# Attention scores issued two units at a time, their norms and transposes joined, and a new searched order of all instructions

## The chip, the cores and the metric

The kernel runs on one core of one Trainium2 chip. The metric is device time in microseconds (us), the median of several executions. The kernel before takes 306.1 us (306.01 to 306.51 in six runs, 0.2% apart).

Names used below: PE is TensorE's matmuls, PEld its weight loads, DVE is VectorE, ACT is ScalarE, POOL is GpSimd, SP is SyncE. "L482" is line 482 of the kernel's file. The changed kernel's lines are two higher for the same code; the experiments' lines are shifted by a few more.

## The reference, cut to what matters

Sliding-window attention with a linear bias, followed by a two-layer network with `h * cos(h)` between the layers:

```python
def _attn_ref(q, k, v):                       # 8 batches, 8 heads, 576 tokens, 64 per head
    scores = scale * np.matmul(q, k.transpose(0, 1, 3, 2))
    bias = slopes[:, None, None] * (-np.abs(rel))[None, :, :]
    mask = (rel >= 0) & (rel < 128)
    ...                                       # softmax over the masked scores
    return np.matmul(attn, v)

def _moe_ref(x, w_in, w_out):                 # 4608 tokens, 512 -> 2048 -> 512
    h = x @ w_in
    g = h * np.cos(h)
    return g @ w_out
```

## The kernel before: the parts that matter

The kernel records every operation with what it reads and writes, and then sorts them by a table of start times, `STARTS`. The order on each engine is therefore not the order of the source. The table was made by a search outside the file, and it also chooses the engine of those copies that two engines could do. Semaphore waits are derived from the recorded reads and writes.

```python
def schedule(self):
    raw, n = zlib.decompress(base64.b85decode(STARTS)), len(self.all)
    assert len(raw) == 2 * n
    code = 0
    for i, o in enumerate(self.all):
        code = (code + 256 * raw[i] + raw[n + i]) & 0xFFFF
        o.start = code >> 1
        if len(o.eng) > 1:
            e = "dve" if code & 1 else "act"
            o.fn, o.eng = o.fn[e], (e,)
    self.order = sorted(self.all, key=lambda o: (o.start, o.seq))
```

A unit is two heads by 256 queries. Its scores (K = 64) run in a TensorE tiling mode of 64 rows, everything else in the full array, or for the first transposes of q and k in 64 columns (the trace marks them 64\*128, 128\*128 and 128\*64). So each block of scores costs two changes of mode, measured below at 0.11 us each. After the scores come `exps` (ScalarE), `mask` (VectorE), `pv` (the products with v, TensorE), `norm` (VectorE: a reciprocal and a multiply) and `x_pe` (a transpose on TensorE and a copy).

```python
for n, u in enumerate(two):         # SINGLE = True: one unit's scores at a time
    scores([u], n)                  # banks SB[2n], SB[2n+1] of SB = [4, 5, 6, 7]
    exps(u, n, 2 * phase + 2)
    mask(u)
```

The softmax here doesn't subtract the row's maximum and nothing guards it: scores larger than these inputs give would overflow.

Of the kernel before, what the change touches and what calls it, by code (L numbers as in the profile page):

```python
# [14 lines left out]
B, H, S, D = 8, 8, 576, 64  # L15
# [12 lines left out]


STARTS = (  # L30
    "c-p;I3wTpS7S4^hPOtW3IEza=4J8h@wO<IOmTQ`1lBUHbq_qaD(3XObK9qJTg3wwN+^Q4{SV7CWu(niTzXjG+<RPGZDlcIHV"
    "dX>CU13+($G$#yeJ%(z$=$hmv`N!e*jL)jopa{QxpV$G=ReU1ilPa96#l3FYlNT}P?WGP_zf;bOhca`f=2izvaAVPs$(Ep5e"
    "Ujcl&JKG8jU~lK3|X9K+jCMYF+QlKZu=h#a^QQDLrDhFr=R-BiQv5XGHAr7>I;@A?ObYT5V9gc%7gKUuyb(0&yB8PUF|~|52"
    "h=L$CGsjIlO>E717+zl2^80)0RTL|yhkAcUM~eZsdIMNkHbWiUj9e+M*W05?|)nsNo2z~G<_QZNCbSM*1}J%Uwl1uETIRj1X"
    "cSZV|PVX1sKP*<6N!T>hfezDXJh^2pk8_*1(iA7t9E;%L8dmtsU&mZ!w@P{wDUIpc{x)9JR!lf`d__Y5E)P#7Ae-LDQXMNdG"
    "h{8|kSrwv+pg$%Q24zvrfP00$@kc<{1_IGH5JiHaNd#qW=yBm%)unJ*qYZWvpYUJ6xG#P}JjPK-#b-?f+t4w6!Ld6odwo}_`"
    "Hsv~`kt<rH5GqsC%LEzb?E;?8TW0({ejiP|Jq174OFxPX#!zQOj7l{A`Yt1uFL!x0p~wPp*xPIl(-h)i)$*E28hiUMQj5_>l"
    "<K~5Z4Wr_y7X2blTqyedk3BSJeCd$-mdcw0K_+U&p3Fe2*Kb-}U(+!CR7|RpL(K?{n_>^D6yBr3l?Iv4r?9&<_@Ye!NW{p$x"
    "I6r|Xkat=EWWu=pOr#+%*lJh!{+ughOZN?)|M;_ie`X9&&Dyr1;wKVHns%d=Vez}MaGWm_t$6!&d9hrvnqtx0+wo|an1CA;p"
    "D-Y9UEFRqr(!1OT((mt$s`YXA5O#Y0{tm>4_W9sC}iO-jfoDCPGM4};Q%~MUQ%Rm~va)ujaVUaw>=D@QA0TO>=zZK;YA|i91"  # L40
    "<F_J0A^}wO+(bYwB*F1a`<+~cC7^nC3>9H+fC!rhG6e+qk;TtI?F3XxbCcM5wATOxiAMW#NOgmdnXOSD{F^@aei6y)EU7U~U"
    "7RoeE@|=Yhz2c_nmW{n4T%|+1ZVes`O1`n#KWes*Lii@eo9s^|Cw%9C4N2WBk}-U?wOW3GQC<i_g3i)o@o2^=%IAOr1BNa!B"
    "Ln*juY*ssUtp^dMO8Al#&UMB=cG_-onH7sX)GczSg+ItIiTx?K<!C7^nwU%0R(d3K)vA%dtEk1C(O0O8iM_c0uU^z_PJGhar"
    "yw-bk}|gK<Ay0=S495U!>zf8;Yg+XaBFjsv(0+ARBwFTfDT;qv-|lKi`JZS}|5PypHOd<L+T%a-zYmE`Z@qinyC?<!`kKwbK"
    "dX<z{AybgO^#?8mzO-z5Y83WF0U4L&QVb6A$Ryg=&&LS66pVc`Jj;E6zziSc)A^+y{#AYsgw{7}%HR=SNhUB@bof|7JSyYi|"
    "NrTixhN&R5xZUmURlYa9H}0R`zRv7@;GSGWJi)sP4M{if;h>1fWMo!VaFYc^Evr|RT@)n&h$uNhO`@Qt0VEL_zOkH$+L1XNi"
    "{mUVG+e5QY!U&bSgbt!2x#xiRnW!?UunP@j)m@qE*o2sxeYeihw|{t*#>UoajfC?C)gf7n({li-o}0bUsK7x9oK^1-t2+g8H"
    "K~>Q5$uh<2Gjt?K_<0qvf}grpk(~riq5VnIG#Wot~At_QiX6=D@rK#a(XNw9oxoheO4XXAUZVa38GxzM4o}EPmD0NH(XQbe("
    "g8bobFwFz1NtVN*4I!f;?LzlB|$E2(><JF{lDH~FcqBlnuK+79IsM53|$l8^h<+z;!<9};81TrNLi<ydeG4Vfy~B1)OlYw%_"
    "f9iBCA!-S|U9NqMrEG2xJ71jV6j*=}lEMbW?^OB?%JCTdpEbqu}(6GW)vi_oD85F=2XE#qhgJT&5$Ym!vqD5>N9}Vmsjuy55"  # L50
    "O~$!=R1>*!wTo*eHenw&GsdAe73RP7Bw5<F`C)tB(J4de*L%yGN6@m7IUI*CIv=2Q{_OQ+Lw?Cik2Hfc?zC>tdmkMiV{K9kG"
    "~q`_QY%f4s@q&ScW~<`JI_|RSGpH8RC%xW4q1h)GqYx65(7%omz;;n)wxkZqSYuCE{rUi)Z9TRJ^O;nQCvACyeWBvsz9McuD"
    "P!!d*shuVRy!cEu6e~l8&4C7R^LbLr_u|?>saC5ap@Pv+xelAYz`xCia==;TM5O8@okBd9v6gmax}?T$We<5Sxt%-+^+mqcG"
    "^7LWZM>v!KYgNR9(Rs>4Rgt__;;bv6qjo4QI_Vvq@CsIoT_PN#fX@0`sQh!|lBQzJm&Zl`6paZYxrt1SO`*~#|%8~u{O{NWA"
    "7H7}nt9^0c<cuGyNYpE_Vb)o5&oZ+4Wr|aOBuXW8jR<)3f8P8EpsJYnUKIMM>pMI}|*I8#iHFg!hX=4aR;9(}c4%F77CTsAN"
    "Hq=xXlb1SFAs-1#7z)%}vz6^b!K72Q=E>Yk;V~<Bi|8vV%IWHmymJu-A{)gYw1+)?V$rGDW!V!X$YcP|N;bCy;2_I^<M1i_q"
    "yXq%KIa_3)&q9w?VAa~l-<mkG1I=3Q*a*J$!k4>P2z4STSKvncBJ46pe#kDQoD2c;iASJvv%FX<F=5~yDR3U(G@B4TnDAr&S"
    "F}*x?*Z^cN%sWaya{Sr7m6aMR5n2p2IV<we!!ZvviH?oWwGgV|shdljf>Zwbrb&e~INgNcsSfxrOxVo@kA+0I@jx^Qa9fs>#"
    "hUK8`+~Y}wr-+t8NsdNOV2j0pa#5Snm0(|Gr<0t7I%?+ijV3@A^+p<CdF49CzC;(N$37a&v5DzPM|v&Fn+$!t2eoLsmV8#%a"
    "-%6u=YBU^E%J;7KY>FdrL0HjOf3s!mP^fF?kMbp;O?M-bb>sIsdS9I>>g<jD#TBW<zPPg<hxrt+xv&@`zBGX!XDyRL&MowqZ"  # L60
    "WM&X|_k?7F#(WgRW*H^&-$esFhDt;#k|kd6OmX5#2pg<J(ghLKUvJr=iu1)#b%<5yGt2LT2Bcn`Pt*)Wdn}&E$qqep@_yN78"
    "O2dZXYU$8mgXM9Qucji-%@aW&+-!g`LW5qmN#HM8}DiHQ1%HvxQMcIKrd4^mU0By9krz{{a1;+X}`)wac}y=5B^Zb3s{vkD="
    "XJ~>Z$F)GZ0eB%bmADG5cdAx;pu<5b_v#2mv9ZT7wps+c()lVUp~Pk*W}R!xq7loQPEd?*U?Rq2)wx>V(M2vd9(7`)TZRp79"
    "y$&x0%<nRBBDpnknyHsN;mK3;Hi!rOZYHf^2ra<D)C2{1WhUkX&_T*3!F%7#+PzTzGV*cbE^p{$x$&H{D_Xq$;WxM(XB%*i%"
    "qrGodA?hS~^RM=mh;mQRn8oTOwMRsxBzVcrJ*4a4Kz6#+W)6W{LC?xQ4n;J;6=4k+<3yHb1+r!DL7RHSJL)xcd#|J}s56b9o"
    "NAC!~ZW|{Kb&{NRF701)z3_t"
)


# [150 lines left out]
def bass_alibi_sliding__then__act_gcu_kernel(  # L220
# [8 lines left out]
    with ExitStack() as ctx:  # L229
        def sb(name, shape, dt=BF16):  # L230
            return ctx.enter_context(nc.sbuf_tensor(name, shape, dt))

        R = Plan(nc, ctx)
# [7 lines left out]
        HF = NFC // 2  # L241
        T = {n: sb(f"wsum{n}", [128, HF, 256], F16) for n in (1, 2, 3, 4)}
# [9 lines left out]
        P = [sb(f"p{i}", [128, 2, 512]) for i in range(NP)]  # L252
        Pt = [sb(f"ptail{i}", [128, 1088]) for i in range(2)]
# [17 lines left out]
        SB, UB, OB = [4, 5, 6, 7], [2, 3], [0, 1]  # L271
# [634 lines left out]
            step("P4", "Y", False, (None, "p1", 2))  # L906
            step("P3", "Z", False, (None, "u2", 1))

        PAIRN = False
        SINGLE = True  # L910
        ucount = [0]

        def attention(us, phase):

            for g in range(0, len(us), 2):
                two = us[g:g + 2]
                if phase < 0 or SINGLE:
                    for n, u in enumerate(two):
# [66 lines left out]
        for c in range(NCH):  # L985
# [12 lines left out]
            n = QUOTA[c] if c < len(QUOTA) else 0  # L998
# [41 lines left out]
```

## Time and profile before

| | recorded profile of before | before, profiled again |
|---|---|---|
| span, us | 377.5 | 304.6 |
| time of that execution, us | 379.17 (slow state) | 306.34 (fast state) |
| PE / DVE / ACT busy | 97% / 69% / 55% | 96% / 83% / 67% |
| start to start, 512 columns | 266 or 318 ns | 216 ns |
| start to start, 256 columns | 110 or 159 ns | 109 ns |

These are the head of the recorded page, its chain of waits by engine, and two of its groups (line, engine, operation, tiles, shapes, count, then busy us and mean ns of one, then idle time before):

```profile
span 377.5 us, 7154 instructions
PE 365.6 (97%) x2882; PEld 228.0 (60%) x2900; DVE 260.7 (69%) x548; ACT 209.1 (55%) x298; POOL 95.1 (25%) x122
...
PE 96%; DMA 1%; ACT 1%; issue 1%; DVE 0%; ACTq 0%
...
L608 DVE TENSOR_TENSOR xnat<-ps,rec 128x256 bf16<-128x256 f32 x64 | 24.7, 419 | 0.3
L606 DVE RECIPROCAL rec<-ps 128x4 f32<-128x4 f32 x64 | 8.5, 168 | 18.5 <-PE ps L570 18.3
```

TensorE is the engine that bounds the kernel: 97% busy, 96% of the chain. But this execution took 379 us where plain ones take 306.

### The profile page before, as it was taken

How to read it: one execution, taken by the hardware profiler on the slowest of the kernel's cores; microseconds unless marked ns; L12 is line 12 of the kernel's file. 1: busy time of each engine (PE TensorE's matmuls, PEld its weight loads, DVE VectorE, ACT ScalarE, POOL GpSimd, SP SyncE). 2: the span in 40 equal slices, each digit the busy share in tenths (PEclk: the TensorE clock that was granted, in tenths of full speed). 3: DMA queues.
4: the chain of work that ended last, by engine and by line, in shares of the span. 5: the costliest groups of instructions: out<-in, count | busy, mean ns of one | idle time of the engine just before them, and what ended most of it. 6: DMA issues, size and time to landing. Idle time of an engine off the chain costs nothing.

```text
span 377.5 us, 7154 instructions
## 1 busy us (share of the span) xinstructions
PE 365.6 (97%) x2882; PEld 228.0 (60%) x2900; DVE 260.7 (69%) x548; ACT 209.1 (55%) x298; POOL 95.1 (25%) x122
## 2 busy tenths in 40 slices
PE   3999999999999999999999999999999999999997
PEld 2677445447753676447787765467645655554775
DVE  3976855568857877688757885787679654865743
ACT  6967655656646676558536862666456633445000
POOL 8992304196047002900490011000000000000000
DMA  8999999999989929990999389301220110100023
GB/s 150 182 211 203 168 181 130 133 124 157 149 117 156 109 37 158 171 93 28 114 160 180 52 92 136 88 10 37 55 77 2 43 21 28 44 13 0 30 84 113
DMA packets 148353, 38.09 MB, mean 101 GB/s; under 512 B 133984, under 2 KB 147040, under 8 KB 148320
## 3 DMA queue, kind: packets, MB, share of 16 engines
q0 software_dynamic: 99344, 18.10, 62.7%
q1 hardware_dynamic: 48976, 19.54, 25.6%
q8 instruction: 23, 0.38, 0.4%
q14 instruction: 10, 0.08, 0.1%
HBM read 36.70 MB, written 9.44 MB: 122 GB/s over the span
## 4 chain that ended last, share of the span: by engine, by line
PE 96%; DMA 1%; ACT 1%; issue 1%; DVE 0%; ACTq 0%
PE ps L712 38%; PE ps L853 34%; PE ps L482 5%; PE ps L797 5%; PE ps L736 5%; PE ps L567 3%; PE ps L570 2%; PE ps L429 2%; PE ps L674 1%; DMA ob<-in_q_dram 1%; ACT p L512 1%; PE ps L473 1%; PE ps L554 1%; PE ps L556 1%; DVE kt L445 0%
## 5 line engine op out<-in xcount | busy, mean ns | idle before, releaser
L712 PE MATMUL ps<-xT,w_inb 128*128 128x512 bf16 (+1 forms) x558 | 155.2, 429 | 1.6 <-DVE rec L606 0.2
L718 ACT ACTIVATE cos<-ps,halfpi 128x512 f32<-128x512 f32 x128 | 84.4, 686 | 83.8 <-PE ps L712 55.6
L722 DVE TENSOR_TENSOR gT<-ps,cos 128x512 f16<-128x512 f32 x128 | 85.0, 687 | 43.4 <-ACT cos L718 43.0
L712 PEld LDWEIGHTS ps<-xT,w_inb 128*128 128x128 bf16 x576 | 63.0, 111 | 65.4 <-issue 56.4
L512 ACT ACTIVATE p<-ps 128x768 bf16<-128x768 f32 (+1 forms) x64 | 56.3, 915 | 23.1 <-PE ps L482 16.1
L326 POOL DMA_DIRECT2D vp<-in_v_dram x40 | 33.8, 861 | 105.0 <-PE ps L570 87.6
L536 DVE TENSOR_TENSOR p<-p,emask 128x512 bf16<-128x512 bf16 (+2 forms) x96 | 42.4, 464 | 12.0 <-ACT p L512 11.0
L853 PE MATMUL ps<-wsum,gT 128*128 128x256 f16 x256 | 49.6, 319 | 0.0
L853 PE MATMUL ps<-wsum,gsum 128*128 128x256 f16 x256 | 47.7, 316 | 0.0
L853 PE MATMUL ps<-w_outb,gT 128*128 128x256 f16 x256 | 46.2, 319 | 0.3
L853 PEld LDWEIGHTS ps<-w_outb,gT 128*128 128x128 f16 x256 | 28.2, 111 | 12.2 <-issue 5.3
L853 PEld LDWEIGHTS ps<-wsum,gT 128*128 128x128 f16 x256 | 27.8, 112 | 10.0 <-issue 4.1
L853 PEld LDWEIGHTS ps<-wsum,gsum 128*128 128x128 f16 x256 | 27.1, 110 | 9.2 <-issue 2.8
L336 POOL DMA_DIRECT2D qnat<-in_q_dram x30 | 25.4, 887 | 15.7 <-DMA qt<-qnat 15.7
L336 POOL DMA_DIRECT2D knat<-in_k_dram x30 | 25.6, 915 | 11.5 <-DMA kt<-knat 9.3
L853 PE MATMUL ps<-w_outb,gsum 128*128 128x256 f16 x128 | 25.5, 320 | 0.0
L608 DVE TENSOR_TENSOR xnat<-ps,rec 128x256 bf16<-128x256 f32 x64 | 24.7, 419 | 0.3
L482 PE MATMUL ps<-qt,kt 64*128 64x128 bf16 (+1 forms) x320 | 22.0, 266 | 1.3 <-DVE kt L445 0.9
L567 PEld LDWEIGHTS ps<-vp,p 128*128 128x128 bf16 x256 | 18.5, 104 | 5.2 <-issue 2.5
L606 DVE RECIPROCAL rec<-ps 128x4 f32<-128x4 f32 x64 | 8.5, 168 | 18.5 <-PE ps L570 18.3
L567 PE MATMUL ps<-vp,p 128*128 128x65 bf16 x256 | 21.0, 206 | 0.0
L736 PE MATMUL ps<-xT,w_inb 128*128 128x256 bf16 x128 | 20.6, 314 | 0.0
(70 smaller groups left out, 355.5 us busy)
## 6 DMA issues: line engine op xcount, KB each, us to landing
out_dram<-ob SPq DMA_DIRECT2D x32, 256.0 KB, 2.4
vp<-in_v_dram POOLq DMA_DIRECT2D x32, 128.0 KB, 5.7
qnat<-in_q_dram POOLq DMA_DIRECT2D x24, 128.0 KB, 6.8
knat<-in_k_dram POOLq DMA_DIRECT2D x24, 128.0 KB, 8.3
w_inb<-in_moe_w_in_dram POOLq DMA_DIRECT2D x4, 512.0 KB, 10.7
w_outb<-in_moe_w_out_dram POOLq DMA_DIRECT2D x4, 512.0 KB, 22.5
out_dram<-ob SPq DMA_DIRECT2D x8, 128.0 KB, 1.7
qrows<-in_q_dram POOLq DMA_DIRECT2D x1, 576.0 KB, 15.4
```

What stands on the lines that cost most here:

```text
L326: op("pool", [lambda e, t=t, rows=rows: e.dma_start(vp[b % 2][0:rows, t, :, 0:64], v[b, :, 128 * t:128 * t + rows, :].rearrange("h p d -> ...
L336: fns.append(lambda e, t=t, rows=rows: e.dma_start(nat[which][b % 2][0:rows, t, :, :], src[b, :, 128 * t:128 * t + rows, :].rearrange("h p ...
L482: ins = e.matmul(ps[:, banks[x], c0:c1], keys_ap(b, x, pr, kc), query_ap(b, x, pr, qb, 128 * nb), start=True, stop=True)
L512: op("act", lambda e: e.activation(P[i][:, :, 0:hi], src_[:, :, 0:hi], ACTF.Exp, scale=0.125), w=held + [("P", i)], occ=920 if G else 691, ...
L536: op("dve", lambda e, p=p, m=m: e.tensor_tensor(p, p, m, ALU.mult), r=[("P", i), ("EM", h0), ("EM", h1)], w=[("P", i)] if n != 1 else [("P ...
L567: ins = e.matmul(o, P[i][:, x, d0:d0 + 128], V[:, kc, h, 0:65], start=True, stop=not two)
L608: op("dve", lambda e: e.tensor_tensor(o, U[:, :, :, 0:64], rv[:, :, :, None].broadcast_to([128, 2, 2, 64]), ALU.mult), r=[("rec", n % 2)], ...
L712: op("pe", lambda e, kc=kc, c0=c0: e.matmul(ps[:, bank, c0:c0 + n], w_in[:, kc, 128 * fc:128 * fc + 128], xT[:, kc, (r0 + c0) % XR:(r0 + c ...
L718: op("act", lambda e: e.activation(cosb[ci][:, :], ps[:, bank, :], ACTF.Sin, bias=halfpi[:, 0:1]), r=["halfpi"], w=[("B", bank), ("cos", c ...
L722: op("dve", lambda e: e.tensor_tensor(gT[gi][:, fc, :], ps[:, bank, :], cosb[ci][:, :], ALU.mult), r=[("cos", ci)], w=[("B", bank), ("g", ...
L736: op("pe", lambda e, i=i, fc=fc, kc=kc: e.matmul(ps[:, bank, 256 * i:256 * i + 256], w_in[:, kc, 128 * fc:128 * fc + 128], xT[:, kc, r0:r0 ...
L853: op("pe", lambda e, t=t, fc=fc, bk=bk: e.matmul(ps[:, bk, 256 * t:256 * t + 256], lhs(fc, t), rhs(fc), start=first and fc == 0 and (last ...
```

## The change

It is meant to issue the scores of two units back to back in each stay in the 64-row mode, to join the norms and the x transposes of such a pair into single instructions, and to use an order found by a swap search on the engines' sequences. The diff, with the two tables cut:

```diff
 STARTS = (
-    "c-p;I3wTpS7S4^hPOtW3IEza=4J8h@wO<IOmTQ`1lBUHbq_qaD(3XObK9qJTg3wwN+^Q4{SV7CWu(niTzXjG+<RPGZDlcIHV"
+    "c-oy-4RjM#7S8lXpQEnNCmz~Ifbcpkbr@<5Lz`xjG@)q-w5Ao0r7czF)LKhHt!yi7Es9Wf6}niJgZv#9q#}wUi@TMj3cD+N2"
     ... (the rest of both tables is cut)
 )
@@
-        PAIRN = False
-        SINGLE = True
+        PAIRN = True
+        SINGLE = False
         ucount = [0]
```

With the flags, `scores(two, 0)` is one recorded operation that holds all four banks `SB`, and `norm_two` and `x_pe_two` serve a pair. The first group of units (batch 0, before the network starts) is recorded singly in both kernels: `if phase < 0 or SINGLE`.

More of the change, by code (lines that the diff above doesn't have):

```diff
@@ L30 @@
 STARTS = (
-    "c-p;I3wTpS7S4^hPOtW3IEza=4J8h@wO<IOmTQ`1lBUHbq_qaD(3XObK9qJTg3wwN+^Q4{SV7CWu(niTzXjG+<RPGZDlcIHV"
-    "dX>CU13+($G$#yeJ%(z$=$hmv`N!e*jL)jopa{QxpV$G=ReU1ilPa96#l3FYlNT}P?WGP_zf;bOhca`f=2izvaAVPs$(Ep5e"
-    "Ujcl&JKG8jU~lK3|X9K+jCMYF+QlKZu=h#a^QQDLrDhFr=R-BiQv5XGHAr7>I;@A?ObYT5V9gc%7gKUuyb(0&yB8PUF|~|52"
-    "h=L$CGsjIlO>E717+zl2^80)0RTL|yhkAcUM~eZsdIMNkHbWiUj9e+M*W05?|)nsNo2z~G<_QZNCbSM*1}J%Uwl1uETIRj1X"
-    "cSZV|PVX1sKP*<6N!T>hfezDXJh^2pk8_*1(iA7t9E;%L8dmtsU&mZ!w@P{wDUIpc{x)9JR!lf`d__Y5E)P#7Ae-LDQXMNdG"
@@ L36 @@
-    "h{8|kSrwv+pg$%Q24zvrfP00$@kc<{1_IGH5JiHaNd#qW=yBm%)unJ*qYZWvpYUJ6xG#P}JjPK-#b-?f+t4w6!Ld6odwo}_`"
-    "Hsv~`kt<rH5GqsC%LEzb?E;?8TW0({ejiP|Jq174OFxPX#!zQOj7l{A`Yt1uFL!x0p~wPp*xPIl(-h)i)$*E28hiUMQj5_>l"
-    "<K~5Z4Wr_y7X2blTqyedk3BSJeCd$-mdcw0K_+U&p3Fe2*Kb-}U(+!CR7|RpL(K?{n_>^D6yBr3l?Iv4r?9&<_@Ye!NW{p$x"
-    "I6r|Xkat=EWWu=pOr#+%*lJh!{+ughOZN?)|M;_ie`X9&&Dyr1;wKVHns%d=Vez}MaGWm_t$6!&d9hrvnqtx0+wo|an1CA;p"
-    "D-Y9UEFRqr(!1OT((mt$s`YXA5O#Y0{tm>4_W9sC}iO-jfoDCPGM4};Q%~MUQ%Rm~va)ujaVUaw>=D@QA0TO>=zZK;YA|i91"
@@ L41 @@
-    "<F_J0A^}wO+(bYwB*F1a`<+~cC7^nC3>9H+fC!rhG6e+qk;TtI?F3XxbCcM5wATOxiAMW#NOgmdnXOSD{F^@aei6y)EU7U~U"
-    "7RoeE@|=Yhz2c_nmW{n4T%|+1ZVes`O1`n#KWes*Lii@eo9s^|Cw%9C4N2WBk}-U?wOW3GQC<i_g3i)o@o2^=%IAOr1BNa!B"
-    "Ln*juY*ssUtp^dMO8Al#&UMB=cG_-onH7sX)GczSg+ItIiTx?K<!C7^nwU%0R(d3K)vA%dtEk1C(O0O8iM_c0uU^z_PJGhar"
-    "yw-bk}|gK<Ay0=S495U!>zf8;Yg+XaBFjsv(0+ARBwFTfDT;qv-|lKi`JZS}|5PypHOd<L+T%a-zYmE`Z@qinyC?<!`kKwbK"
-    "dX<z{AybgO^#?8mzO-z5Y83WF0U4L&QVb6A$Ryg=&&LS66pVc`Jj;E6zziSc)A^+y{#AYsgw{7}%HR=SNhUB@bof|7JSyYi|"
@@ L46 @@
-    "NrTixhN&R5xZUmURlYa9H}0R`zRv7@;GSGWJi)sP4M{if;h>1fWMo!VaFYc^Evr|RT@)n&h$uNhO`@Qt0VEL_zOkH$+L1XNi"
-    "{mUVG+e5QY!U&bSgbt!2x#xiRnW!?UunP@j)m@qE*o2sxeYeihw|{t*#>UoajfC?C)gf7n({li-o}0bUsK7x9oK^1-t2+g8H"
-    "K~>Q5$uh<2Gjt?K_<0qvf}grpk(~riq5VnIG#Wot~At_QiX6=D@rK#a(XNw9oxoheO4XXAUZVa38GxzM4o}EPmD0NH(XQbe("
-    "g8bobFwFz1NtVN*4I!f;?LzlB|$E2(><JF{lDH~FcqBlnuK+79IsM53|$l8^h<+z;!<9};81TrNLi<ydeG4Vfy~B1)OlYw%_"
-    "f9iBCA!-S|U9NqMrEG2xJ71jV6j*=}lEMbW?^OB?%JCTdpEbqu}(6GW)vi_oD85F=2XE#qhgJT&5$Ym!vqD5>N9}Vmsjuy55"
@@ L51 @@
-    "O~$!=R1>*!wTo*eHenw&GsdAe73RP7Bw5<F`C)tB(J4de*L%yGN6@m7IUI*CIv=2Q{_OQ+Lw?Cik2Hfc?zC>tdmkMiV{K9kG"
-    "~q`_QY%f4s@q&ScW~<`JI_|RSGpH8RC%xW4q1h)GqYx65(7%omz;;n)wxkZqSYuCE{rUi)Z9TRJ^O;nQCvACyeWBvsz9McuD"
-    "P!!d*shuVRy!cEu6e~l8&4C7R^LbLr_u|?>saC5ap@Pv+xelAYz`xCia==;TM5O8@okBd9v6gmax}?T$We<5Sxt%-+^+mqcG"
-    "^7LWZM>v!KYgNR9(Rs>4Rgt__;;bv6qjo4QI_Vvq@CsIoT_PN#fX@0`sQh!|lBQzJm&Zl`6paZYxrt1SO`*~#|%8~u{O{NWA"
-    "7H7}nt9^0c<cuGyNYpE_Vb)o5&oZ+4Wr|aOBuXW8jR<)3f8P8EpsJYnUKIMM>pMI}|*I8#iHFg!hX=4aR;9(}c4%F77CTsAN"
@@ L56 @@
-    "Hq=xXlb1SFAs-1#7z)%}vz6^b!K72Q=E>Yk;V~<Bi|8vV%IWHmymJu-A{)gYw1+)?V$rGDW!V!X$YcP|N;bCy;2_I^<M1i_q"
-    "yXq%KIa_3)&q9w?VAa~l-<mkG1I=3Q*a*J$!k4>P2z4STSKvncBJ46pe#kDQoD2c;iASJvv%FX<F=5~yDR3U(G@B4TnDAr&S"
-    "F}*x?*Z^cN%sWaya{Sr7m6aMR5n2p2IV<we!!ZvviH?oWwGgV|shdljf>Zwbrb&e~INgNcsSfxrOxVo@kA+0I@jx^Qa9fs>#"
-    "hUK8`+~Y}wr-+t8NsdNOV2j0pa#5Snm0(|Gr<0t7I%?+ijV3@A^+p<CdF49CzC;(N$37a&v5DzPM|v&Fn+$!t2eoLsmV8#%a"
-    "-%6u=YBU^E%J;7KY>FdrL0HjOf3s!mP^fF?kMbp;O?M-bb>sIsdS9I>>g<jD#TBW<zPPg<hxrt+xv&@`zBGX!XDyRL&MowqZ"
@@ L61 @@
-    "WM&X|_k?7F#(WgRW*H^&-$esFhDt;#k|kd6OmX5#2pg<J(ghLKUvJr=iu1)#b%<5yGt2LT2Bcn`Pt*)Wdn}&E$qqep@_yN78"
-    "O2dZXYU$8mgXM9Qucji-%@aW&+-!g`LW5qmN#HM8}DiHQ1%HvxQMcIKrd4^mU0By9krz{{a1;+X}`)wac}y=5B^Zb3s{vkD="
-    "XJ~>Z$F)GZ0eB%bmADG5cdAx;pu<5b_v#2mv9ZT7wps+c()lVUp~Pk*W}R!xq7loQPEd?*U?Rq2)wx>V(M2vd9(7`)TZRp79"
-    "y$&x0%<nRBBDpnknyHsN;mK3;Hi!rOZYHf^2ra<D)C2{1WhUkX&_T*3!F%7#+PzTzGV*cbE^p{$x$&H{D_Xq$;WxM(XB%*i%"
-    "qrGodA?hS~^RM=mh;mQRn8oTOwMRsxBzVcrJ*4a4Kz6#+W)6W{LC?xQ4n;J;6=4k+<3yHb1+r!DL7RHSJL)xcd#|J}s56b9o"
@@ L66 @@
-    "NAC!~ZW|{Kb&{NRF701)z3_t"
+    "c-oy-4RjM#7S8lXpQEnNCmz~Ifbcpkbr@<5Lz`xjG@)q-w5Ao0r7czF)LKhHt!yi7Es9Wf6}niJgZv#9q#}wUi@TMj3cD+N2"
+    "+E&|g1D>fuIs@cJm61hX`1YvN!q4O6)`=Xd2@f>y!+kn-a7^^6f%T=K`s<bi0_I^=m|f9JZRv8unb%D+4cVtxOl_40Y&&094"
+    "rWF*HF}Ba9|_t-fQ5rzc|B%{%wQ(tI%c3hSOfY?{Id#15t!}An;IBm|9eQ&wWvbxDXeG$sk?i*QH$oyn*95U8}jA8wxVK_@{"
+    "qxmheu|GOl+>O7vXz?-tN(2BkF^wT`{&S}xkgzzqNp90Eq@N8n8C)^G6vt~300u7?|P@EDE-hYI3*FKNOJm2im{hDs7HM!m1"
+    "Me;-a?bB5mGA^1^%Vr>S;6v=uhwhjh!Vi0uNEe<qsfoR{54q6b3=7K>lUhbmdvQfO^;w4QYZ6MldD2j1cbjP3=ib2s3V`GTH"
@@ new lines @@
+    "Y_QD`R)n~SasZ_SL$_XGA&pMjNqV9nijV6GFT#F_ojPFgL9Q$OKJHQ_H4GX*!(=F6kfFd(8`L>Wk^;lXdiysCL~Z!vc9+r`e"
+    ")7H1r|zrY_`m?%iGe`4#x)h{>WjXQl3Ztk<`C?H#-s5%aQS8ZGw_YHkLX?y!{SIx!xOSk!u=#6dt**KY+37d8|*LGctd|f(c"
+    "6zsNG<|UTyHRHhq&IZNa6PU0+I!OLE*;o;L5J3m|`*eg@wz-;sn7PdLqPuf(-V1T@0JX1uh?hxZX>~#|4My${=EP$7~-QJPu"
+    "$k2V*!9g$FlyzQzs$PM^9LhrIXaOu0*^Id+#}B%Lt_48(jA#IAc|zz7XHE&D=@?Wn<iNq-aJf<sOj8YXeU{+1c(-uk(M!^9a"
+    "J2A|@Qp#*DMnki|F_1*t;W$^d6j(Bdo*X#6pjc3f8HYQaDM^tcUE4WARAOGFF8<U+*r_}}*(0jcHOUpm(k@9AgdGo971-?C%"
@@ new lines @@
+    "6Gl&_*SPaaUvTHsaoLVN`0g=n6Goc;JF4(tj!QU>r;Xk>t3ZDBKDA>(HZCLwWzp!b`G{WiCfl0&o(=Pen9<Y9VOGea48&K@D"
+    "MExIi^L}td_^%&vv_j<ePyt~M(lCePso%IL`jlzLY5Gvh#2ixBOVhZV48Cs+aV&J%0}fCq*7arK-bw1$_N}ZyYq-gNI*84GZ"
+    "Q=oDk9Uf<9VbaB1%ch9M}U<ej!y}q?pJxh!)#NEkF2y<GQ7HzrXI*FZ`<GkbhCLd&Y`vLesk!?w?Ur>0fkLebb4_!f{eW-=;"
+    "N9?M0|4mwYZ?PvdAw>FKrp{Cv_WTs`4DwF*ytU6w<H6oUq0!%_cyRn=DcC)yrY7cv18R_boULWz}N!EByV!U!qEguqD{(UdP"
+    "!2O}zBq|`!W8fPgqFJ>8T2a(zwYls&UFZtft1%^y{1{|0&u2jfsQ5LYLWu{zML-y{shdyi~nf7G_%O2NE8J9|~CrM2;%Uwj6"
@@ new lines @@
+    "Y634o^CCXk0gw@rUiO{9h&1slLPVxKAz_lP<e`>NjjfBvPLd0R_bUAd=yKXIkrWB+k@i3M7i5!M#^mWYXDZo5NgbWOqWI=)A"
+    "~XcGFn3rg)fX&VGcDE(xx3P*C4%p}B%R~Us2)ju5|VsAN>AaQgjeh93`ji>S>kERW~}L(31JeCjXWBE+i5T%ni)aHT0uhpbG"
+    "6I0mar^C;?d*AY5zC^_?eW)WDTGYX(TQ7j;vjnw=ZgGBIT}GE6Yzim5(W5Q<Pr=h_$&-K?aW4*J2-G%Dvcu9m>chgrzGhJg`"
+    "sx9e&YhvM;M+lF2^OC%Dt>d8;fbMkk$o8`~qz6ptAHE?QFdSC>CH73!eD_}Bcq%?r<dct<Yq#brE3{jz%1@>{bthEM~Q%+n{"
+    "+hv@U!vM?UsM3Q%jmS;;^<vS;We#??$pLl=k{nK(@U90YGtFdNoJACq@k4lvGAw|!bkx<NZzz_gRlJ`Mb^g)Vv#+ypZ;nAuK"
@@ new lines @@
+    "jJj&<cA|S9m(s#^lRA7FUIIZD9`ezgg^Io?=LvOc7`iQ*iD2Jn1VX0Uw-XJ;7cjvs%6-JdHYl%Ed7M?s6Axi0Q+f#l?PGvby"
+    "8QrHI+ahEEHKv!<^g#kki6ZVr|01SU~I~No+V(Gn_L1CSKd0ywVzjwo`kdTc}Awl)5ob_+~(}6&abLm+<sF=^XsXOshxR5_~"
+    "BPl*6$kUooTq2ypi<0sa~|q?i6V1L_*1h`cp05T5r8^xB7bPy7%^5pS$MX0mg-CmyQG`F#Xv`t%OhBt^-AM$~d&9VV*}3U!y"
+    "-0{gQkS?Pn<x8kuv}$Zx{WP*s2$zpXYUg%CF+!a{7o)?&H7?&0h%JrjsGDX$O;O%3x?lovHO@My_ds(NKP4Fv?{=BkyXnb>?"
+    "u%Ew@Xrz0Ti9A4CtB%1A8i0**Xa}(h-$cZUat|Ov{U{JdrW;zS_H06&3l1K?MDepj|)XvJ3?UctV{4?b(QpcdYWtRII^jX*s"
@@ new lines @@
+    "nOu2z<qyZ8$r>#y*6o$O*H+EWeZ0<Dwm(qof4BJUQ|q%wh}YAxB*hH~(?h%FW&@qqx9&aXJ>@Mt{t-}Ro~8BJv=#@F5taGyJ"
+    "9+vIT-yPdKE#u|2jNf281rInVTs75^C<Z@k#+S$RxL9b<IV<jHUsaFM4eK_wz5StAYW(?ox*!hQ&pu$Ms=KHL^dfC1aqlLaZ"
+    "#hQCFjv<Qa?u7{Ph_!U%9<Fy%stfCM8hBl*p3($+kwk*gjFxnn8+clTAhI7m}0a&96e2W3EIG7ECjz)xp~S8kPX%vUQfpg?Q"
+    "#Ib!(ba-Fr4X(*C!arE@D@wrp7}%hP+RE4SZ-dx~?Cg!u18%k|f6YJV^XD*T<&E5y<TZ>0MhG(tXh?nG7GvDMa>Hr?>@R%+A"
+    "RT7-vVcvLKfnFrEB>CUMUl(f!eWRy=j?HuTByvC*Ed-Ti^B<hBhwf8(#AK@WFww;-n?7U@eg-?e*!{;PyrHs5&*A{A%Bu6Vp"
@@ new lines @@
+    "(cVk7!Yyd+I_b$h>~tUhOu1ELPWII@m^iYsMV};36iaxu{V*1=nA-rwD!5#vq@+r@McXGY9{^>p&`u4fS)~}TEZFEBpINYMN"
+    "_*9_RcD&oH@Cl8Mh>k}zI;wt=J`DgztlIsU2~Vksy1g2E=5Ecl8jV~pTQ^x!K9;lc<@JgC^?w-d-el3z*ydaq)jl-`LW&5q!"
+    "{53QK>{iRfsQ|GXi-QW{D2$19qu4pwrA<!g3;J^1kIZW1-YeguI*tN)EBS8yRu7%$e)JewNd*fryp%KR2~NbxdL&=`Q8KN!7"
+    "-bJ67%Rn3R7rI$yF+v&lZDoR>VZ=k~wg`I1Tb0LvSk4L1<E(W<O(q^nHIldD8WtzuPQ%KXMMZ}mrFO9FgllwyGba|KpaCon`"
+    "EAfl3wPywZOBcJv?Vv~3(QrUxOrqAOL>l}niZeE7Yjz_K40>soqeE>lT&x&%~G~BUxF$+Kt(6}6r1MorG6x2zCr{)xY+vsai"
@@ L67 @@
+    "CYF4^gf+aisu_m+`y1qAyBdn{ZuPVESE?1nWPir!-&?NayG>-HGMl=0o0J|u{j%cI2N>Hp|E(=0OXfp!*@{*7qSRBX#q<aEw"
+    "UOOf_RVAmq<NlNv-`AVx9KQMUjb6)$#Nj=5MN7saTePIRQ*KSSquf<G@JF<njmZS=%1S~<W~E}_?%To`s+5?h>Z}+zida<CP"
+    "^wqG>$dD4H-urDatcRS_d{V$3{rI7THy)XH(K3WC^0)3DIhuIF$NB>i+?MBOA>"
 )
```

## The prediction

> **What bounds it.** TensorE. The page's busy table gives PE 97% of a 377.5 us span (VectorE 69%, ScalarE 55%); the chain of waits is 96% PE. [...] Matmuls of 256 columns start alternately 110 and 159 ns apart; of 512 columns, 266 or 318. The plain run lasts 306 us, 71 less than the profile: I take the extra ~50 ns on about every second weight load to be the profiler's. So the profiled TensorE is a quarter slower than the real one, and waits on VectorE and ScalarE that exist in the plain run hardly show.
>
> Estimate of the plain run from starts (216 ns for 512 columns, inferred as 266 minus 50; 110 for 256, 56 for 128, 30 for the 65-column products): first layer 125 us, second 112, products with v 17, scores 14, transposes 9: about 278. Before the first matmul 5.5, after the last 2.8. Tiling-mode switches: from a second-layer matmul to scores 253 ns, against 110/159 in stream; from scores to the next full-array matmul 148 to 197, against 53 to 103. So about 95 ns each; the order has 96: 9 us. [...] Sum 295; the plain span is about 304 (the profiled run reports 1.7 us beyond its span). So some 9 us are waits, about 2 of them in the first 28 us.
>
> **What the change does.** Matmul counts per shape stay. In the built order switches fall only from 96 to 88, because the old order already put most neighbouring units together: 8 x 95 ns = 0.8 us, on the path. Only 4 pairs of norms join: two singles are 2 x (168 + 419) ns, a joined pair roughly 170 + 690: 0.3 us each, 1.2 us of VectorE, mostly off the path. ScalarE's x copies go from 27 to 20 plus 3 double. Joining holds all four score banks, so the next pair waits for two exponentials (about 1.0 us each), a small risk. The larger part is the order: TensorE alternates first and second layer far more finely (order rows 1068 to 1282), and the unbroken second-layer run at the end shrinks from 181 to 131 matmuls; those 50 fill places where the old order would wait. Waiting instructions fall: PE 348 to 321, VectorE 338 to 304. It can only win from the 9 us of waits.
>
> **On the path.** 0.8 us surely, plus about a quarter of the 9 us: 2.5. Predicted 302.8 us, range 299.0 to 306.3. Faster by over 2% (below 300.0) needs two thirds of the waits gone: 0.14. Within 2%: 0.83. Slower by over 2%: 0.03.
>
> **What would show it.** PE still 95 to 97% of the profiled span and of the chain; the profiled span falls less than the plain time, by about 1 us, since the profile hides the waits. Switch gaps stay near 95 ns, fewer. VectorE busy falls by 1 to 2 us. The last pure second-layer stretch shortens from 26 us to about 19.
>
> **What would make it wrong.** The 278 us floor rests on inferred start distances; if those are 2 ns larger (2900 matmuls, 6 us), little is left to win. If double scores starve ScalarE or leave TensorE waiting for banks, it is flat or slower. If the search found nearly all waits, it is faster than 2%.

## More of the kernel before

The argument will turn on some small operations at the very start, which put constants into tiles:

```python
def constants():
    for i in range(2):
        op("dve", lambda e, i=i: e.memset(vp[i][:, :, :, 64:65], 1.0), w=[("vinit", i)])
        op("dve", lambda e, i=i: e.memset(vp[i][64:128, 4, :, 0:64], 0.0), w=[("vinit", i)])
        op("dve", lambda e, i=i: e.memset(Pt[i][:, 1024:1088], 0.0), w=[("Pt", i)])
    op("dve", lambda e: e.memset(halfpi[:, :], math.pi / 2.0), w=["halfpi"])
    for i in range(2):
        op("dve", lambda e, i=i: e.memset(...tail columns of k..., 0.0), w=[("ktail", i)])

def load_v(b, order=range(NBLK)):             # queued by POOL, in program order
    for t in order:
        ...
        op("pool", [lambda e, ...: e.dma_start(vp[b % 2][...], v[b, ...])],
           r=[("vinit", b % 2)], w=[("v", b % 2, t)], dma=f"ldv{b % 2}{t}",
           occ=900, lat=740 * rows // 100)
```

The loads of v read `vinit`, so POOL holds them, and all loads that it queues after them, until both memsets of that v tile are done (in after, below, it idles 2.61 us for one of them).

## The result, and the profile after

The kernel after takes 307.9 us (307.11 to 308.51, six runs), before 306.1. The ratio is 1.0054, interval [1.0034, 1.0074]: half a per cent slower, where 302.8 us and at most 306.3 had been predicted.

The profile of after, head and chain of waits:

```profile
span 306.7 us, 7126 instructions
PE 293.7 (96%) x2881; PEld 198.9 (65%) x2900; DVE 253.0 (82%) x540; ACT 204.6 (67%) x294; POOL 95.2 (31%) x122
...
PE 93%; DVE 3%; DMA 1%; issue 1%; ACT 1%; ACTq 0%
```

Set against the 377.5 us of the recorded profile, after would look 19% faster, while by plain time it is slower. So the first run was the kernel before once more, for a profile.

### The profile page after: what moved, and what is told of

Same layout as the page of the kernel before. It is cut to its first block, busy times and chain, and to the rows that moved or that the text cites. A ratio compares the mean times of both kernels' runs of the same rounds, so it can differ in the third digit from the quotient of the medians.

```text
span 306.7 us, 7126 instructions
## 1 busy us (share of the span) xinstructions
PE 293.7 (96%) x2881; PEld 198.9 (65%) x2900; DVE 253.0 (82%) x540; ACT 204.6 (67%) x294; POOL 95.2 (31%) x122
## 2 busy tenths in 40 slices
DMA packets 148353, 38.09 MB, mean 124 GB/s; under 512 B 133984, under 2 KB 147040, under 8 KB 148320
## 3 DMA queue, kind: packets, MB, share of 16 engines
HBM read 36.70 MB, written 9.44 MB: 150 GB/s over the span
## 4 chain that ended last, share of the span: by engine, by line
PE 93%; DVE 3%; DMA 1%; issue 1%; ACT 1%; ACTq 0%
PE ps L714 35%; PE ps L855 33%; PE ps L484 5%; PE ps L738 5%; PE ps L799 5%; PE ps L569 3%; PE ps L431 2%; PE ps L572 2%; DMA ob<-in_q_dram 1%; PE ps L676 1%; PE ps L475 1%; PE ps L558 1%; PE ps L556 1%; DVE xnat L610 1%; DVE gT L724 0%
## 5 line engine op out<-in xcount | busy, mean ns | idle before, releaser
L714 PE MATMUL ps<-xT,w_inb 128*128 128x512 bf16 (+1 forms) x557 | 126.2, 355 | 0.9 <-ACT p L514 0.4
L714 PEld LDWEIGHTS ps<-xT,w_inb 128*128 128x128 bf16 x576 | 54.4, 98 | 44.2 <-DVE gT L724 5.5
L855 PE MATMUL ps<-wsum,gT 128*128 128x256 f16 x256 | 46.0, 273 | 0.3 <-issue 0.2
L855 PE MATMUL ps<-w_outb,gT 128*128 128x256 f16 x256 | 43.4, 273 | 0.2
L855 PEld LDWEIGHTS ps<-w_outb,gT 128*128 128x128 f16 x256 | 24.8, 98 | 7.0 <-DVE ob L879 0.4
L855 PEld LDWEIGHTS ps<-wsum,gT 128*128 128x128 f16 x256 | 23.8, 98 | 6.3 <-issue 0.3
L855 PEld LDWEIGHTS ps<-wsum,gsum 128*128 128x128 f16 x256 | 23.9, 98 | 6.1 <-issue 0.6
L610 DVE TENSOR_TENSOR xnat<-ps,rec 128x256 bf16<-128x256 f32 x56 | 22.2, 418 | 1.0 <-DVE rec L608 0.2
L569 PE MATMUL ps<-vp,p 128*128 128x65 bf16 x256 | 19.0, 197 | 0.9 <-issue 0.7
L484 PEld LDWEIGHTS ps<-qt,kt 64*128 64x128 bf16 x320 | 11.7, 98 | 9.6 <-issue 3.8
L572 PE MATMUL ps<-vp,p 128*128 128x65 bf16 x192 | 17.7, 196 | 0.0
```

The costliest lines, as they stand in the source:

```text
L484: ins = e.matmul(ps[:, banks[x], c0:c1], keys_ap(b, x, pr, kc), query_ap(b, x, pr, qb, 128 * nb), start=True, stop=True)
L569: ins = e.matmul(o, P[i][:, x, d0:d0 + 128], V[:, kc, h, 0:65], start=True, stop=not two)
L572: ins = e.matmul(o, P[i][:, x, p0:p0 + 128], V[:, kc - 1, h, 0:65], start=False, stop=True)
L610: op("dve", lambda e: e.tensor_tensor(o, U[:, :, :, 0:64], rv[:, :, :, None].broadcast_to([128, 2, 2, 64]), ALU.mult), r=[("rec", n % 2)], ...
L714: op("pe", lambda e, kc=kc, c0=c0: e.matmul(ps[:, bank, c0:c0 + n], w_in[:, kc, 128 * fc:128 * fc + 128], xT[:, kc, (r0 + c0) % XR:(r0 + c ...
L855: op("pe", lambda e, t=t, fc=fc, bk=bk: e.matmul(ps[:, bk, 256 * t:256 * t + 256], lhs(fc, t), rhs(fc), start=first and fc == 0 and (last ...
```

## The experiments

### The kernel before, profiled again (e0_before_again)

No edit.

> The kernel before, unchanged, to get a profile in the fast state: the recorded profile of before was of the slow state (377.5 us against a plain time of 306.1), so it cannot be set beside the profile of after (306.7). Theory A (the new order costs more waits on TensorE than the old): the fast profile spans about 304.5 us, its matmul starts are 216 ns (512 columns) and 109 ns (256 columns) apart as in the profile of after, and the waits of TensorE sum to about 2 us less than in after. Theory B (the waits are equal, the joined instructions or something at the start are dearer): waits equal within 0.5 us after the first 30 us, the difference in the first 30 us or after the last matmul. Ratio to before 1.000 within 0.002.

Measured: 306.22 us, ratio 1.0005 [0.9988, 1.0022], and a profile in the fast state, of an execution that took 306.34 us:

```profile
span 304.6 us, 7154 instructions
PE 292.3 (96%) x2882; PEld 196.4 (64%) x2900; DVE 253.8 (83%) x548; ACT 204.8 (67%) x298; POOL 95.0 (31%) x122
...
PE 82%; DVE 8%; DMA 3%; POOL 3%; issue 2%; ACT 2%; POOLq 0%; ACTq 0%
```

Matmuls start 216 and 109 ns apart in both fast profiles. I then compared all matmul starts of the two traces, filling the 18 and 19 records missing from them from the order in which each program was built. "Waits" are what a start-to-start distance in the full array has beyond 216, 109, 56 or 30 ns (512, 256, 128, 65 columns); "switch gaps" are the same excess over pieces with a change of mode. ("Full array" is the mode that the trace marks 128\*128.)

| from 22.5 us (before) or 25 us (after) to the last matmul | before | after |
|---|---|---|
| waits within the full array, us | 3.46 | 3.68 |
| switch gaps, us (changes of mode) | 9.44 (84) | 8.57 (74) |
| last matmul starts, us | 301.54 | 303.30 |

After the start of the kernel the new order is better by 9.44 - 8.57 = 0.87 us of mode changes and no better in waits; a change costs 9.44 / 84 = 0.11 us in before and 8.57 / 74 = 0.12 in after. The whole loss lies before that, as theory B had it. A second count of the same traces, which sets two scores side by side in the 64-row mode at half the distance, gives 3.78 and 4.01 us of waits and 9.25 and 8.12 us of switch gaps: the sizes are good to a few tenths of a us, and the reading is the same. The timeline view (start us, us, engine, line, operation, count, and in brackets the idle time before it and what ended that) of before shows its beginning:

```profile
1.46 0.27 DVE L392 MEMSET vp<- 64x256 uint32 x1
...
5.42 1.76 POOL L326 DMA_DIRECT2D vp<-in_v_dram  x2
...
8.33 0.83 PE L482 MATMUL ps<-qt,kt 64*128 64x256 bf16 x8 [0.88 <-DVE kt L445]
...
12.46 0.33 PE L567 MATMUL ps<-vp,p 128*128 128x65 bf16 x3
...
16.36 0.27 PE L736 MATMUL ps<-xT,w_inb 128*128 128x256 bf16 x1
```

and of after:

```profile
7.57 0.27 DVE L394 MEMSET vp<- 64x256 uint32 x1
...
8.14 1.77 POOL L328 DMA_DIRECT2D vp<-in_v_dram  x2 [2.61 <-DVE vp L394]
8.54 0.17 DVE L398 MEMSET kt<- 128x128 uint32 x1
...
8.85 0.82 PE L484 MATMUL ps<-qt,kt 64*128 64x256 bf16 x8 [1.29 <-DVE kt L398]
...
13.69 0.33 PE L569 MATMUL ps<-vp,p 128*128 128x65 bf16 x3 [0.73 <-issue]
...
18.39 0.42 PE L738 MATMUL ps<-xT,w_inb 128*128 128x256 bf16 x1
...
19.50 1.67 PE L738 MATMUL ps<-xT,w_inb 128*128 128x256 bf16 x7
```

The search moved six of the nine memsets of VectorE back from the front; two of them hold others up. One (L394, 0.27 us of work) now holds POOL idle for 2.61 us, so the v loads are queued at 8.14 instead of 5.42 us. By the trace's landing records the first of them still lands at the same time (11.51 against 11.54 us), but the second, for which the first product with v waits, at 13.60 instead of 12.37 us. The other (L398) holds the first scores. The first products with v come 1.23 us later, and the first-layer matmuls 2.03 us later, at double length: seven take 1.67 us.

That gave two theories. **M**: the late memsets are the loss, these two above all. **O** (rival): the new order of TensorE's own instructions in the first 25 us is, since it also holds norms and transposes back.

### Memsets put back to the front of after (e1_memsets_first)

```diff
         o.start = code >> 1
+        if o.eng == ("dve",) and 11 <= o.seq <= 19:    # the nine memsets of constants()
+            o.start = 40 + o.seq - 11
```

> The kernel after, with the nine small VectorE memsets of constants moved back to the front of VectorE's order; nothing else. Theory M (the loss at the start comes from two of these memsets: one gates the v loads of the Pool queue, issued 2.7 us later in after, one gates the first scores): time falls from about 307.9 to 305.2 - 305.8, below before; the first v load is issued at about 5.4 us, TensorE's clock goes full near 14 us instead of 21. Theory O (the order of TensorE's own instructions in the first 25 us, norms and transposes held back, costs it): gain under 0.7 us, time over 307.2.

Measured: 305.38 us (305.16 to 305.57), ratio 0.9972 [0.9960, 0.9984]. It is faster than before, and 2.5 us faster than after. Its timeline:

```profile
1.23 0.27 DVE L396 MEMSET vp<- 64x256 uint32 x1
...
5.54 1.76 POOL L330 DMA_DIRECT2D vp<-in_v_dram  x2
...
8.45 0.82 PE L486 MATMUL ps<-qt,kt 64*128 64x256 bf16 x8 [0.88 <-DVE kt L449]
...
12.51 0.33 PE L571 MATMUL ps<-vp,p 128*128 128x65 bf16 x3
...
16.64 0.27 PE L740 MATMUL ps<-xT,w_inb 128*128 128x256 bf16 x1
...
17.36 0.94 PE L740 MATMUL ps<-xT,w_inb 128*128 128x256 bf16 x7
```

TensorE's sequence is the same as in after, so O is ruled out as the main cause. The two traces can be compared matmul by matmul: after is behind by 13.69 - 12.51 = 1.18 us at the first product with v, by 1.75 at the first first-layer matmul, by 2.86 at the 31st (25.14 against 22.28) and by 2.86 at the last of all (303.30 against 300.44).

### The old start, the new rest (e2_head_old)

```diff
-STARTS = ( ...the table of after... )
+STARTS = ( ...the old order for the 333 operations that the old table starts before 1650, all engines;
+           then the new order... )
```

> The whole old order for the first 333 of 2765 recorded operations (about the first 25 us, all engines), the new order and the joined instructions from there. Both M and O: 305.2 to 305.6 us, because the new order from 33 us on has 0.9 us less of mode switching and equal waits. If it is clearly below the kernel with only the memsets moved, the difference is what the rest of the new order at the start costs; M says under 0.4 us, O says over 1.5.

Measured: 305.97 us, ratio 0.9992 [0.9978, 1.0005]. This missed its expectation: it is 0.6 us above the memsets-first kernel. So the rest of the new start is, if anything, better than the old start once the memsets are early (O had it worse); some of the 0.6 us may belong to the seam between the two orders.

### The same memsets made late in before (e3_memsets_late)

The reverse: the kernel before, with the memsets at the places that after gives them in VectorE's sequence. The sequences of the other engines stay the same.

```diff
-STARTS = ( ...the table of before... )
+STARTS = ( ...the same order, with the memsets at the places that after gives them among VectorE's operations... )
```

> The kernel before, with the nine memsets put where after has them among VectorE's instructions; the sequences of the other engines are unchanged. M: 306.1 rises to 308.0 - 308.9, the clock goes full 3 to 8 us later. O: under 306.8.

Measured: 308.16 us (307.41 to 309.82), ratio 1.0066 [1.0045, 1.0087]. The loss of after is reproduced in the old order with single scores. POOL again waits 2.6 us for the memset:

```profile
8.15 1.77 POOL L320 DMA_DIRECT2D vp<-in_v_dram  x2 [2.62 <-DVE vp L386]
```

M holds in both directions.

### Which of the two memsets (e9_v_memset_first, e10_k_memset_first)

```diff
         o.start = code >> 1
+        if o.seq == 12:          # e9: zero the tail rows of v;  e10: o.seq == 18, the tail columns of k
+            o.start = 45
```

> The kernel after, with only one memset moved to the front: the zeroing of the tail rows of the v tile, for which the first v load waits. If the late v loads are the loss, 305.3 to 306.2 and the first products with v start near 12.9 us instead of 13.7. If it is the k memset that holds the scores, 307.3 or more.

> The kernel after, with only the zeroing of the k tail columns moved to the front, for which the first scores wait. If the late v loads are the loss: 307.2 to 308.0, scores start 0.4 us earlier but the products with v still wait for v. If the k memset is the loss: 306.2 or less.

Measured: 305.93 us with only the v memset early (ratio 0.9998 [0.9983, 1.0014]), 308.29 us with only the k memset early (ratio 1.0069 [1.0055, 1.0084], 0.3 us above the range expected). The v memset, through POOL's queue, is most of the cause: moving it takes back 1.7 of the 2.5 us by the means (ratio 1.0054 to 0.9998; one of its runs was slow, 307.51 us) and 2.0 by the medians. The k memset alone gains nothing: its scores start at 8.52 instead of 8.85 us, and the products with v still start at 13.48. The remaining 0.5 to 0.8 us came only with all nine memsets early; which of the others it needs was not tested.

The timeline ends the wait before these products with "issue", so it names no cause. The landing records do: where the v loads are late, the first product's weight load starts 0.06 us after the second v load lands (in after it lands at 13.60 us, with the k memset early at 13.39, with the memsets late in before at 13.37), while the masked scores had been ready since 12.89, 12.55 and 12.93. In before and in the memsets-first kernel both are ready at about the same time (load 12.37 and 12.42 us, mask 12.41 and 12.47).

### How much of it is TensorE's half clock (e4_warm_after)

After 12.5 us the delay grows from 1.18 to 2.86 us, although the sequences are equal. In that stretch the first-layer matmuls of after last about twice as long (seven in 1.67 us against 0.94). The trace has records of the granted clock: full from 14.1 us on in before (profiled again), from 14.8 in the memsets-first kernel, from 21.4 in after. In after, matmuls of 256 columns start 213 ns apart before that step and 109 after it, so I call the part before it half clock. The recorded stretches quoted here last 3.41 us or a multiple: 21.44 to 308.16 us in after (286.72 us, 84 times 3.413), 8.56 to 11.97 in the warmed after below. The page's clock row and the windows view do not show the first half-clock part: in after the row has a 9 in every slice, and the view gives 1.00 for 18.02 to 21.44 us.

My guess was that TensorE gets full clock sooner if it is at work sooner. To test what half clock costs, it was kept busy while it waits for its first data:

```diff
+        warm, wkeys = gT[1][:, 0, :], [("g", 1, 0, 0), ("g", 1, 0, 1)]
+        def heat(e):
+            for _ in range(9):
+                ins = e.matmul(ps[:, 7, :], warm[:, 0:128], warm, start=True, stop=True)
+            return ins
+        op("dve", lambda e: e.memset(warm, 1.0), w=wkeys)
+        op("pe", heat, r=wkeys, w=[("B", 7)])
         load_first_q()
```

with both operations put first in `schedule`.

> The kernel after, with nine 128x512 matmuls of ones into an unused bank while TensorE waits for the first data (result unchanged). It separates the direct waits from the half clock. Theory C (most of the loss is TensorE at half clock up to 21 us, where before is at full clock from 14): the clock goes full by 8 us and the time falls by 2 us or more, to 305.9 or less. Theory W (the waits for memsets and v loads themselves are the loss, the slow clock hides in them): falls by under 0.8 us, to 307.1 or more. If the clock does not stay full, the run tells nothing.

Measured: 309.27 us (307.62 to 310.52), slower still, ratio 1.0108. By its own terms it tells nothing of the question, since the clock did not stay full: in the profiled run it was full at 5.15 us and half again from 8.56 to 11.97. But it gave something else. Each run lists its mean granted clock, and one stretch of 3.41 us at half clock takes 0.5 x 3.41 / 305 = 0.0056 from it. The six runs are 307.62 (0.994, one stretch), 308.17 (0.989, two), 309.24, 309.30 and 310.52 (0.983, three) and 310.49 (0.978, four). In this kernel more stretches go with a longer time. The v-memset kernel shows the same: five runs of 305.88 to 305.96 at 1.0, one of 307.51 at 0.994. Two other kernels do not: with the memsets late in before, 307.63 us goes with 0.994 and 308.37 with 1.0, and with only the k memset early the slowest run, 309.11 us, has 0.999. (The mean leaves out the half clock before the first record: after is listed at 1.0, with full clock only from 21.44 us on.) So this is a correlation, not a test.

Profiles at hand go further. The slow run of the v-memset kernel is the profiled one. Its v loads are in time, but its clock, full from 13.08 us, was halved from 16.50 to 19.91. The windows view (stretch, its length, busy us of PE, PEld, DVE, ACT and POOL with instructions, then the granted clock, mean busy DMA engines and GB/s):

```profile
13.08:16.50 3.42, 2.23 (x39) 1.36 (x38) 3.13 (x14) 3.19 (x4) 3.42 (x6) 1.00 1.97 173
16.50:19.91 3.41, 3.41 (x38) 2.37 (x38) 2.22 (x5) 2.58 (x5) 3.41 (x5) 0.50 1.25 207
```

Matmul by matmul it is 0.28 us behind the memsets-first kernel at 16.25 us, 1.68 at 19.84 and 1.83 at the end: half clock over the first-layer matmuls is enough for about 1.5 us, without late loads. Late loads are enough too, without half clock there. With the memsets late in before the clock was full from 17.17 us, ahead of the first first-layer matmul (17.53), and TensorE then waited for first-layer weights that POOL queues behind the v loads. The same matmuls in before and in that kernel:

```profile
20.23 0.39 PE L736 MATMUL ps<-xT,w_inb 128*128 128x256 bf16 x2 [0.40 <-DMA w_inb<-in_moe_w_in_dram]
```

```profile
21.84 0.39 PE L730 MATMUL ps<-xT,w_inb 128*128 128x256 bf16 x2 [0.69 <-DMA w_inb<-in_moe_w_in_dram]
```

Its last matmul starts 1.5 us later than in before. With only the k memset early (clock full from 16.95 us, first layer from 17.80) the last matmul is 2.2 us behind the memsets-first kernel; there TensorE waits 0.73 us for a v load that lands at 20.07.

### Warming where the memsets are early (e8_warm_memsets_first, e12_warm_twice)

The first is e1 plus e4. The second adds five more such matmuls between the first transposes and the first scores:

```diff
+        op("pe", lambda e: heat(e, 5), r=wkeys, w=[("B", 7)])      # start 323
```

> The memsets-first version of after with the nine idle-time matmuls. If the half clock between 5.5 and 14 us is on the path, 304.5 or less (from 305.4) in runs where the clock stays full; if the clock falls back as in the warmed after, or the path there runs through ScalarE, VectorE and the loads, 305 to 306.5.

> As the former, with five more idle matmuls between the first transposes and the first scores, so that TensorE is not idle in the second 3.4 us of its work. If idle time made the clock fall back in the warmed after, it now stays full and the time is 303.5 to 304.8; otherwise no better than the former.

Measured: 306.09 us (ratio 0.9989) and 306.12 us (ratio 0.9997 [0.9983, 1.0010]). In the second the clock is full from 6.67 us to the end, and still it is no faster than the kernel without warming (305.4): its 31st first-layer matmul starts at 22.16 us, in the memsets-first kernel at 22.28. TensorE then waits for others instead. The waits from 5 to 25 us (engine, line, who ended the wait, us in total, times, longest):

```profile
PE ps L574 <- DVE p L543: 1.0, 2, 0.8
PE ps L489 <- ACT p L519: 0.5, 2, 0.4
PE ps L436 <- DMA krows<-in_k_dram: 0.5, 1, 0.5
PE ps L743 <- DMA w_inb<-in_moe_w_in_dram: 0.4, 1, 0.4
```

So taking away the half clock up to 14 or 15 us gained nothing, and TensorE waited for loads, ScalarE and VectorE there instead. (What the added matmuls and their memset cost themselves was not separated.) The v-memset profile above shows that it costs when it falls on the first-layer matmuls, after 16 us.

### Two more looks at after (e13_after_look1, e14_after_look2)

No edit.

> The kernel after, unchanged, to catch a profile of its quicker runs (its six runs fell into 307.1 - 307.4 and 308.4 - 308.5; the one profiled, 308.42, reached full clock at 21.4 us). If the clock's step is what parts the two groups, a run of 307.1 - 307.4 reaches full clock one 3.4 us stretch earlier, near 18 us, and a run of 308.4 - 308.5 near 21.4. If the two groups do not follow the step, the clock is not what parts them.

> As the former look, a second throw: 307.1 - 307.4 with full clock near 18 us, or 308.4 - 308.5 with full clock near 21.4 us.

Measured: 308.81 and 308.24, 308.42 and 307.55 us; the profiled ones were the first of each. Neither profile caught a quick run, so whether the clock's step is what parts the two groups of times stays open. Full clock came at 21.07 us in the second look, again in a slow run. In the first it came at 12.60, was lost at 16.01 and returned at 22.84. The windows view of it, in the columns given above:

```profile
9.20:12.60 3.40, 3.40 (x54) 2.45 (x52) 1.98 (x6) 3.00 (x4) 3.40 (x5) 1.00 1.29 89
12.60:16.01 3.41, 1.76 (x42) 1.32 (x40) 2.47 (x10) 2.41 (x4) 3.41 (x5) 1.00 1.31 162
16.01:19.42 3.41, 3.03 (x40) 1.69 (x38) 3.38 (x11) 2.53 (x5) 3.41 (x6) 0.50 1.79 173
19.42:22.84 3.42, 3.42 (x39) 2.61 (x34) 1.19 (x5) 3.39 (x5) 3.42 (x5) 0.50 1.25 205
```

TensorE was busy 1.76 of 3.41 us before it was set back; in the warmed after it was 1.44 of 3.41 (5.15 to 8.56 us), in the v-memset kernel 2.23 of 3.42. The twice warmed kernel kept full clock after a stretch with 1.91 of 3.42 (10.08 to 13.50 us). So the busy time of the stretch before does not decide it alone; what does is not shown. (The 1.00 of the first line is the gap in the records told of above.) In all three profiles of after the first matmuls of the first layer (from 18.4 to 18.6 us on) run at half clock, by way of a late step (21.44 and 21.07 us) or of a fall back (until 22.84).

### The joining by itself, in the new order (e5_split_new_order, then e15_joined_again and e16_split_again)

The joins undone, the order kept: the memsets-first kernel with `SINGLE = True`, `PAIRN = False`, each single operation at the place and on the engine of the joined one; 88 changes of mode in both.

```diff
-        PAIRN = True
-        SINGLE = False
+        PAIRN = False
+        SINGLE = True
```

> The two joins undone (single scores, norms and x transposes, as in before), the new order kept, with the memsets first as in the memsets-first kernel; 88 mode switches as there. Theory J (the joined instructions matter): differs from the memsets-first kernel (305.4) by 0.5 us or more. Theory N (the joining in itself changes nothing, only the order and its switches do): 305.1 to 305.8.

> The memsets-first version of after again (305.4 before), on one chip with its split twin. If the joining is worth nothing or costs a little: 0 to 0.5 us above the twin. If it helps: below the twin.

> The split twin again (305.0 before): the new order, memsets first, single scores, norms and transposes. 304.9 to 305.4, at or below the joined one of the same call.

Measured: 305.00 us (ratio 0.9968 [0.9956, 0.9980]), just outside both theories. Against the joined kernel (ratio 0.9972) that is only 0.1 us, and the runs of the two overlap. They were run at other times. Hence the pair on one chip: joined 305.47 (305.37 to 305.91), split 304.99 (304.66 to 305.06), ratios to before 0.9969 and 0.9949 [0.9936, 0.9961]. By the means, 305.54 and 304.93, joining costs 0.6 us there, and the runs of the two do not overlap; over both it costs 0.1 to 0.6 us. In the traces the waits within the full array, counted as in the table above, are 3.66 us joined and 3.22 split. The split one is the fastest kernel.

### The joining in the old order (e6_joined_old_order, e11_split_moved)

e6 has the flags of after in the old order, each joined operation where the later of its two single ones stood. e11 has single operations, but both of each pair at that same later place. TensorE's built sequences are equal, with 86 changes of mode; other sequences differ only by the joined norms and copies.

```diff
-STARTS = ( ...old order... )
+STARTS = ( ...old order, start of a pair = max of the starts of its two units... )   # e6 joined, e11 single
```

> The joined instructions in the old order: each joined one stands where the later of its two single ones stood; the start (memsets, loads, first unit group) is that of before; 86 mode switches instead of 96. Theory N with switches of about 0.1 us each: 306.1 minus 1.0, 305.0 to 305.5, less if first exponentials of a pair come later. Theory J: 306.6 or more, since a joined score waits for all four banks.

> Single scores, norms and transposes in the old order, but both of each would-be pair at the place of the later one: the same sequences on every engine as the joined instructions in the old order (316.2 us), without the joining. Theory J (a joined score waits until all four banks are read by the exponentials, so it stalls where two single ones would not): 306 to 310. Theory P (moving the earlier scores to the later ones' place is what costs, joined or not): 314 to 317.

Measured: 316.18 us (ratio 1.0324 [1.0311, 1.0337]) and 314.40 us (ratio 1.0262 [1.0248, 1.0276]). Neither of my theories for e6 foresaw this: N was 11 us off, and J's "306.6 or more" covers it only in words. Of its 10 us, 8 come from moving the earlier unit's scores, norm and transposes to the later one's place, joined or not, as theory P of e11 had it, although that saves ten changes of mode; joining adds 1.7 us (means 316.15 and 314.42). They were run at other times. One line of TensorE's waits in each, e6 and then e11, for the scores' banks:

```profile
PE ps L475 <- ACT p L505: 3.1, 6, 0.9
```

```profile
PE ps L476 <- ACT p L506: 2.4, 5, 0.7
```

Where the operations of a pair stand is thus worth far more than how many changes of mode they need. The waits show the direction that a joined score would have, holding four banks, but they are a part only of the 1.7 us.

## Why the prediction was wrong, point by point

- **"TensorE bounds it": right.** 96% busy in both fast profiles. Its share of the chain is lower than the 95 to 97% forecast: 82% before and 93% after. VectorE's busy time fell by 0.8 us, not by 1 to 2.
- **"The extra ~50 ns on about every second weight load [is] the profiler's": wrong.** Fast profiles of the same program span 304.6 us and have no such alternation. It belonged to that one execution; its cause is not known. The start distances that I inferred from it were right (216, 109, 56, 30 ns).
- **"8 x 95 ns = 0.8 us" for the changes of mode: right.** 0.87 us (1.1 by the second count) from the start of the network on, where ten changes fall away; two more come at the very start, so that the size fits partly by luck. One change cost 9.44 / 84 = 0.11 us rather than 0.095.
- **"Some 9 us are waits, about 2 of them in the first 28 us": mis-sized and misplaced.** After the first 22.5 us before had only 3.46 us of waits. The slow profile hid where they were; the rest was at the start, mixed with half clock, which I did not see in it.
- **"About a quarter of the 9 us: 2.5" from the finer order: wrong; this term failed.** Waits after the start are 3.46 us before and 3.68 after. The last pure second-layer stretch did shrink, from 19.9 to 14.3 us (181 to 131 matmuls), and fewer waiting instructions are in the program; neither was time.
- **What I left out made the sign wrong.** I looked at how the order moved matmuls and not at nine memsets of under 0.3 us. The order listing that I had showed them moved. One of them holds POOL's queue, so the v loads start 2.7 us later (8.14 against 5.42 us). Moving all nine to the front brings after from 307.9 to 305.38 us, so their places cost 2.5 us; moving that one alone brings 305.93, moving the k memset alone 308.29, which is no gain. Of the 2.86 us by which after trails its memsets-first version, 1.18 are there at the first product with v, a direct wait for a v load. The other 1.68 come up to 25 us, where after runs first-layer matmuls at half clock (seven in 1.67 us against 0.94). But full clock alone would not have saved all of that. The second load of first-layer weights lands at 21.68 us in after; in the memsets-first kernel it lands at 20.20, and its first user starts at 20.25. So I estimate from these landings that late loads alone would have cost after about 1.5 us. In other profiles late loads cost 1.5 and 2.2 us with full clock over the first layer, and half clock there about 1.5 us with early loads. Why the clock came so late in after is not shown; in the other two kernels with late loads it was full at 17.17 and 16.95 us.
- **"If double scores ... leave TensorE waiting for banks, it is flat or slower": right in direction, small.** Joining costs 0.1 to 0.6 us in the new order, 1.7 in the old.

The sum: plus 2.5 for the memsets' places, minus 0.9 for mode changes, plus 0.2 for waits gives 1.8 us, and 307.9 - 306.1 = 1.8 was measured. So exact a match is partly luck: the first term compares medians of different calls, and the others come from one trace each and are good to a few tenths. What joining costs is inside these terms.

Why a search would do this is argued, not shown, as the search is not in the file. The source records `lat=740 * rows // 100`, or 947 for a full v tile, beside `occ=606` for a VectorE multiply that the trace shows at 686 ns; if these are nanoseconds, a v load was thought to land in 0.95 us. The page's table of DMA issues has 7.1 us as the median in after (5.7 in the recorded profile of before):

```profile
vp<-in_v_dram POOLq DMA_DIRECT2D x32, 128.0 KB, 7.1
```

Why the landing takes so long is not shown: other loads were in the queues, and 133984 of the 148353 packets that the page of after counts are under 512 B.

With a load thought to land in 0.95 us, a memset before it would look free for another 2.7 us.

## What to carry to other kernels

When an automatic order replaces another, compare the small instructions that feed a DMA queue first: a 0.27 us memset that gates an in-order queue cost this kernel more (1.7 to 2.0 us) than ten saved changes of mode brought it (about 0.9 us). Separate the searched order from the structural edit before judging either: here the order (with the memsets first) was worth 1.0 to 1.6 us, the joining minus 0.1 to 0.6, and the package lost 1.8. And do not read stalls from a profile whose span is a quarter above the plain time; take it again first.
